# Where in a step the maxima are transposed: one reordering in a fused attention and gated-MLP kernel

## The chip, the cores and the metric

The kernel runs on one core of one Trainium2 chip. The metric is the time of one execution on the device, in microseconds (us), as the median of several runs. A profile is one further execution, recorded instruction by instruction. The engines of the core are named as the profile names them: PE is TensorE (matmuls; PEld is its loading of weights), DVE is VectorE, ACT is ScalarE, POOL is GpSimd, and SP is SyncE, which here only issues DMAs.

## What is computed

Two layers run one after the other, for 8 batches of 576 tokens. The first is a linear attention with 8 heads of 64 channels and 128 learned features, whose features are exponentials made stable by the largest absolute projection of each token. The second is a gated MLP, whose gate mixes the tokens of a batch with a 576 x 576 matrix. This is the reference, cut to its core:

```python
def phi(x):
    proj = np.einsum('bhsd,df->bhsf', x, w_phi)
    proj = proj - np.max(np.abs(proj), axis=-1, keepdims=True)
    return np.concatenate([np.exp(proj), np.exp(-proj)], axis=-1)
q_p, k_p = (phi(q), phi(k))
kv = np.einsum('bhsf,bhsd->bhfd', k_p, v)
z = np.sum(k_p, axis=2)
num = np.einsum('bhsf,bhfd->bhsd', q_p, kv)
den = np.einsum('bhsf,bhf->bhs', q_p, z)[..., None] + 1e-06
attn = num / den            # then heads are joined: x is (8, 576, 512)
...
h = np.maximum(x @ w_in, 0.0)
u, v = (h[..., :d_ff // 2].copy(), h[..., d_ff // 2:].copy())
v_n = (v - mu) / np.sqrt(var + 1e-06)          # mean and variance over channels
v_s = np.einsum('ts,bsd->btd', w_spatial, v_n) + b_spatial[None, :, None]
out = (u * v_s) @ w_out
```

## The kernel before

**Units and steps.** The work of the attention is cut into 36 units. 32 of them are pairs of heads of one batch (4 pairs for each of 8 batches), over the first 512 tokens. The last 64 tokens of a batch, its tail, are handled for two batches at once; such a tail unit holds all eight heads of both batches, and there are four. The program is software-pipelined: `step(i)` runs one stage each of several units. `LAGS` says how many steps after its own number a unit reaches a stage: keys and queries in its own step, the maxima's transpose one step later, features and sums two steps later, attention three, output four. `at_work(what)` finds the units that are due, and `run` calls the stage's functions for them.

**The stages that matter here.**

- `p_queries` projects the queries token by token into two PSUM tiles `pq`, and `r_queries` (line 299) reduces them to the maxima `mq`. GpSimd splits each maximum into a high and a low bf16 part in `mhl` (lines 304 and 305; in the first five units VectorE does it).
- `a_max_t` (line 334) transposes `mhl` on TensorE into a PSUM tile `pt`, and VectorE copies that to `mT` (line 337), so that the maxima lie along the free dimension.
- `p_features` (line 257) starts the feature tiles `pf`: eight small matmuls spread the negative maxima from `mT` with the selection matrix `sel`, and two larger ones add the projected queries. `e_features` (line 277) turns `pf` into `qf` with four exponentials on ACT.
- `p_keys`, `r_keys` and `e_keys` do the like for the keys: `pk`, the maxima `mk` (line 286) and the exponentials `kf` (line 291). `a_scale` makes `em` and, on GpSimd, the scaled values `vs`.
- `a_kv` sums keys times values (`pv<-vs,kf`, 20 matmuls), `a_num` multiplies features with these sums (`pn`) and normalizes them to `x` (lines 359 and 360), and `a_x_t` transposes `x` to `xT`, by TensorE for the first and last units and by DMA for the others.

**The second layer** comes in tasks, which `b_tasks` lists for a finished batch: `b_v` and `b_v_tail` (value half of the MLP, with its statistics), `b_ln`, `b_u` and `b_u_tail` (gate half), `b_s` and `b_s_tail` (mixing of tokens; the eviction multiplies into `uT` or, for the tail, `uTt`, lines 495 and 510), and `b_o` and `b_o_tail` (output projection `po`, evicted to `ob` at line 517 and stored). The tasks wait in a queue, and `fill(0.25)` takes some of them at four places of each step. What is left when the steps are over is run as a drain.

**What sets the order.** From step 8 on (`STRICT`), TensorE's instructions keep the order of the program; before that, and on the other engines throughout, the framework's scheduler orders them. All PSUM tiles come from one pool of eight, and each needs the eviction of an earlier tile of its bank. In a step of the kernel before, the features' matmuls come first, and the maxima's transpose for the next step's features is the last thing; the two stand next to each other in TensorE's queue.

All PE instructions carry the line of one helper, line 62, in the profile, so they are told apart by the names of their tiles.

Of the kernel before, what the change touches and what calls it, by code (L numbers as in the profile page):

```python
# [16 lines left out]
def kernel(  # L17
# [41 lines left out]
    strict = [False]  # L59
# [139 lines left out]
    def transpose_spatial(i):  # L199

        pt = psum.tile([P, S], BF16, tag="bank", name="pt")
        if i < NB:
            sc = POS[i]
            for tp, c in enumerate(POS):
                transpose(out=pt[:, tp * P:(tp + 1) * P], in_=wsp[:, c, bass.ds(sc, P, step=NB)],
                                    identity=ident)
            transpose(out=pt[:, T0:S], in_=wspt[:, bass.ds(sc, P, step=NB)],
                                identity=ident[:TL, :TL])
            nc.vector.tensor_copy(out=w_spT[:, i, :], in_=pt)
            return  # L210
        for bl in range(2):
            lo = bl * TL
            for tp, c in enumerate(POS):
                transpose(out=pt[lo:lo + TL, tp * P:(tp + 1) * P], in_=wspr[:, c, :], identity=ident)
            transpose(out=pt[lo:lo + TL, T0:S], in_=wspt[:, T0:S], identity=ident[:TL, :TL])
            nc.vector.tensor_copy(out=w_spT[lo:lo + TL, NB + bl, :], in_=pt[lo:lo + TL, :])
        for bl, row in ((0, TL), (1, 0)):
            r = slice(row, row + 1)
            pin(nc.scalar.copy)(
                out=w_spT[r, NB + bl, 0:T0].rearrange("o (a b p) -> o a b p", a=2, b=2),  # L220
                in_=bsp_row[r, 0:T0].rearrange("o (p b a) -> o a b p", a=2, b=2))
            pin(nc.scalar.copy)(out=w_spT[r, NB + bl, T0:S], in_=bsp_row[r, T0:S])
# [215 lines left out]
    def b_v(b, j):  # L438
        d = st[b]
        if j == 0:  # L440
            d["vn"] = s2.tile([P, NB, HALF], BF16, tag="vn", name="vn", bufs=2)
            d["uT"] = s2.tile([P, KC, T0], BF16, tag="uT", name="uT", bufs=2)
            d["mv"] = small.tile([P, NB, 2], FP32, tag="mv", name="mv")
            d["vr"] = {}
        d["vr"][j] = s2.tile([P, HALF], BF16, tag="vr", name="vr", bufs=5)
        stats = small.tile([P, 6], FP32, tag="stats", name="stats")
        v_mm(lambda kc: d["xT"][:, kc, j * P:(j + 1) * P], d["vr"][j], slice(0, P), stats, d["mv"][:, j, :])

    def b_ln(b):
        d = st[b]  # L450
        rstd = root(d["mv"], slice(0, P), NB)
        for j in range(NB):
            normalize(d["vn"][:, j, :], d["vr"][j], rstd[:, j, :])

    def b_v_tail(g, bls):
        d = gs[g]
        r = slice(bls[0] * TL, (bls[-1] + 1) * TL)
        vr = s2.tile([P, HALF], BF16, tag="vr", name="vr", bufs=5)
        stats = small.tile([P, 6], FP32, tag="stats", name="stats")
        mv = small.tile([P, 1, 2], FP32, tag="mv_t", name="mv_t")  # L460
        v_mm(lambda kc: d["xTt"][:, kc, r], vr, r, stats, mv[:, 0, :])
        rstd = root(mv, r, 1)
        for bl in bls:
            r = slice(bl * TL, (bl + 1) * TL)
            normalize(vnt[g % 2][r, bl, :], vr[r], rstd[r, 0, :])

    def b_u(b, dc):
        d = st[b]
        pu = psum.tile([P, T0], FP32, tag="bank", name="pu")
        for kc in range(KC):  # L470
            matmul(out=pu, lhsT=w_in_bf[:, kc, dc * P:(dc + 1) * P], rhs=d["xT"][:, kc, :],
                             start=(kc == 0), stop=(kc == KC - 1))
        nc.scalar.activation(out=d["uT"][:, dc, :], in_=pu, func=AF.Relu, bias=0.0, scale=1.0)

    def b_u_tail(g, bls):
        d = gs[g]
        if "uTt" not in d:
            d["uTt"] = s2.tile([P, KC, P], BF16, tag="uTt", name="uTt")
        r = slice(bls[0] * TL, (bls[-1] + 1) * TL)
        pu = psum.tile([P, KC, P], FP32, tag="bank", name="pu")  # L480
        for dc in range(KC):
            for kc in range(KC):
                matmul(out=pu[:, dc, r], lhsT=w_in_bf[:, kc, dc * P:(dc + 1) * P],
                                 rhs=d["xTt"][:, kc, r], start=(kc == 0), stop=(kc == KC - 1))
        nc.scalar.activation(out=d["uTt"][:, :, r], in_=pu[:, :, r], func=AF.Relu, bias=0.0, scale=1.0)
# [26 lines left out]
    def o_mm(lhs, r):  # L512
        po = psum.tile([P, DM], FP32, tag="bank", name="po")
        for dc in range(KC):
            matmul(out=po[r], lhsT=lhs(dc), rhs=w_out_bf[:, dc, :], start=(dc == 0), stop=(dc == KC - 1))
        ob = s2.tile([P, DM], FP32, tag="ob", name="ob", bufs=4)
        (nc.scalar.copy if drain[0] else nc.vector.tensor_copy)(out=ob[r], in_=po[r])  # L517
        return ob

    def b_o(b, j):  # L520
        ob = o_mm(lambda dc: st[b]["uT"][:, dc, j * P:(j + 1) * P], slice(0, P))
        dst = bass.AP(tensor=out.tensor, offset=out.offset + b * S * DM + POS[j] * DM, ap=[[NB * DM, P], [1, DM]])
        nc.sync.dma_start(out=dst, in_=ob)

    def b_o_tail(g, bls):
        r = slice(bls[0] * TL, (bls[-1] + 1) * TL)
        ob = o_mm(lambda dc: gs[g]["uTt"][:, dc, r], r)
        for bl in bls:
            nc.sync.dma_start(out=out[2 * g + bl, T0:S, :], in_=ob[bl * TL:(bl + 1) * TL, :])
# [20 lines left out]
    def b_tasks(b):  # L550

        g, bl = b // 2, b % 2
        alone = g in SPLIT
        bls = [bl] if alone else [0, 1]
        tail = alone or bl == 1
        mm = KC * T0 / 2400.0
        ms = (KC + 1) * T0 / 2400.0
        ts = []
        if tail:
            ts.append((mm, lambda: b_v_tail(g, bls)))  # L560
        ts += [(mm, lambda j=j: b_v(b, j)) for j in range(NB)]
        ts.append((0.0, lambda: b_ln(b)))
        if b == 0:
            ts += [(0.3, lambda i=i: transpose_spatial(i)) for i in range(NB + 1)]
        ts += [(mm, lambda dc=dc: b_u(b, dc)) for dc in range(KC)]
        if tail:
            ts.append((mm * len(bls) / 2, lambda: b_u_tail(g, bls)))
            for x in bls:
                ts += [(ms, lambda dc=dc, x=x: b_s(2 * g + x, dc)) for dc in range(KC)]
            ts.append((ms * len(bls) / 2, lambda: b_s_tail(g, bls)))  # L570
            ts.append((mm, lambda: b_o_tail(g, bls)))
            for x in bls:
                ts += [(mm, lambda j=j, x=x: b_o(2 * g + x, j)) for j in range(NB)]
        return ts

    RATE = 3.35
# [5 lines left out]
    def fill(share):  # L582
        credit[0] = min(credit[0] + RATE * share, CAP)
        while queue and credit[0] >= queue[0][0] / 2:
            cost, task = queue.pop(0)
            task()
            credit[0] -= cost
# [3 lines left out]
    def lag(u, what):  # L591
        return (FT if u["i"] == 1 else FIRST if u["pair"] and u["b"] == 0 else LAGS).get(what, 0)

    def step(i):

        if i == 0:
            a_transpose(units[0])

        def at_work(what):
            return [u for u in units[max(0, i - 5):i + 2] if u["i"] + lag(u, what) == i  # L600
                    and (u["pair"] or what not in ("sums", "attention", "out"))]

        def run(what, *fs):
            for u in at_work(what):
                for f in fs:
                    f(u)

        strict[0] = i >= STRICT
        run("features", p_features)
        run("keys", p_keys)  # L610
        run("queries", p_queries)
        run("features", e_features)
        run("keys", r_keys, lambda u: e_keys(u, 0))
        fill(0.25)
        run("queries", r_queries)
        run("keys", lambda u: e_keys(u, 1), a_scale)
        fill(0.25)
        for u in at_work("attention"):
            a_num(u)
            if u["pj"] == NP - 1:  # L620
                finish_batch(u, tail_num)
        fill(0.25)
        run("sums", a_kv)
        run("next", a_transpose)
        fill(0.25)
        for u in at_work("out"):
            a_x_t(u)
            if u["pj"] == NP - 1:
                finish_batch(u, tail_x_t)
                queue.extend(b_tasks(u["b"]))  # L630
        run("maxima", a_max_t)

    def finish_batch(u, f):
        g, bl = u["g"], u["b"] % 2
# [70 lines left out]
```

## Time and profile before

| what | value |
| --- | --- |
| time, median of 3 runs | 322.27 us (321.13 to 323.19) |
| span of the profiled execution | 320.2 us |
| granted TensorE clock, mean | 0.952 |
| PE, DVE, ACT, POOL busy | 79%, 68%, 67%, 56% |
| transposes of the maxima, mean | 36 of 225 ns |
| copies to `mT`, median | 36 of 211 ns |
| exponentials `qf<-pf` | 144 of 618 ns |

Busy shares are means over a program with several stages: loads and the first steps up to about 55 us, the main loop to about 276 us, and a drain after it. For a change in the order of instructions, the waits tell more than the shares: which engine stood idle, ahead of which instruction, and whose result ended that. The start of `pf` marks the start of a step in the timeline, so that the trace can be cut there and each step be read by itself.

The profile shows the exponentials of the features like this (busy us, mean ns of one, then the idle time of ACT just before them and what ended it):

```profile
L277 ACT ACTIVATE qf<-pf 128x512 bf16<-128x512 f32 x144 | 74.8, 618 | 61.3 <-PE pf L62 61.3
```

### The profile page before, as it was taken

To read this page: it belongs to the slowest core of one execution; us is meant where nothing else is said; L and a number is where in the kernel's file an instruction comes from. 1 tells how busy PE (TensorE), PEld (TensorE's weight loads), DVE (VectorE), ACT (ScalarE), POOL (GpSimd) and SP (SyncE) were. 2 spreads that over 40 slices of the span, in tenths; PEclk is the share of its full clock that TensorE was granted. 3 is DMA by queue.
4 is the path that set the end of the run, shared out by engine and by line. 5 is a ranking of instruction groups with operands and counts; after the bars stand their busy time and mean duration, and the time that the engine had idled before them with its cause. 6 is when DMAs were issued, how large, how long until landed. Compare 5 with 4: busy or idle time off the path is not lost.

```text
span 320.2 us, 8370 instructions
## 1 busy us (share of the span) xinstructions
PE 253.0 (79%) x3270; PEld 158.3 (49%) x3270; DVE 217.3 (68%) x538; ACT 215.3 (67%) x488; POOL 180.6 (56%) x320
## 2 busy tenths in 40 slices
PE   2174768989788697987787888858988878999984
PEld 1063656556445354654654556534455545644541
DVE  4377786876757765878777778857777674875420
ACT  5667876879535786878898867745989853256123
POOL 8259578487513569437968983643598640018400
PEclk9999797979959899999899999998999999999999
DMA  7959999941907729997990899599700000520017
GB/s 194 212 100 185 205 211 128 145 133 14 121 17 194 87 51 218 137 264 179 112 165 18 188 151 191 147 266 230 101 19 18 16 18 23 203 74 2 0 42 253
DMA packets 81707, 40.32 MB, mean 126 GB/s; under 512 B 50243, under 2 KB 77059, under 8 KB 81669
## 3 DMA queue, kind: packets, MB, share of 16 engines
q1 hardware_dynamic: 54180, 28.32, 40.1%
q0 software_dynamic: 27328, 11.41, 31.6%
q8 instruction: 25, 0.41, 0.6%
q14 instruction: 14, 0.11, 0.1%
q10 hardware_dynamic: 160, 0.07, 0.1%
HBM read 32.85 MB, written 9.44 MB: 132 GB/s over the span
## 4 chain that ended last, share of the span: by engine, by line
PE 42%; DVE 23%; ACT 20%; DMA 7%; issue 4%; POOL 3%; SPq 0%; DVEq 0%; ACTq 0%; POOLq 0%
PE ps L62 11%; ACT qf L277 10%; PE pf L62 7%; PE pv L62 7%; PE po L62 6%; ACT kf L291 6%; PE pu L62 5%; DVE stats L421 4%; DMA q_tl<-in_q_dram 4%; DMA out_dram<-ob 3%; DVE mk L286 3%; DVE x L360 3%; PE pn L62 2%; DVE ob L517 2%; DVE uT L495 2%
## 5 line engine op out<-in xcount | busy, mean ns | idle before, releaser
L277 ACT ACTIVATE qf<-pf 128x512 bf16<-128x512 f32 x144 | 74.8, 618 | 61.3 <-PE pf L62 61.3
L315 POOL TENSOR_TENSOR vs<-v_f,em 128x512 bf16<-128x512 f32 x64 | 65.9, 1042 | 50.3 <-ACT em L310 48.7
L291 ACT ACTIVATE kf<-pk 128x512 bf16<-128x512 f32 x144 | 79.3, 663 | 4.3 <-DVE mk L286 4.2
L286 DVE TENSOR_REDUCE mk<-pk 128x4 f32<-128x512 f32 x72 | 46.4, 686 | 36.5 <-PE pk L62 34.3
L62 PE MATMUL pf<-mT,sel 64*128 64x128 bf16 x288 | 15.6, 232 | 39.7 <-DVE mT L337 38.4
L299 DVE TENSOR_REDUCE mq<-pq 128x4 f32<-128x512 f32 x62 | 40.5, 680 | 0.1
L62 PE MATMUL ps<-w_spT,vn 128*128 128x512 bf16 (+1 forms) x256 | 38.8, 286 | 1.4 <-POOL vn L435 1.0
L62 PEld LDWEIGHTS <-sel 64*128 64x128 bf16 x288 | 10.2, 99 | 47.6 <-DVE mT L337 28.3
L421 DVE BATCH_NORM_STATS2 stats<-vr 128x6 f32<-128x512 bf16 (+1 forms) x37 | 25.0, 684 | 11.9 <-ACT vr L420 11.7
L62 PE MATMUL pv<-w_in_bf,xT 128*128 128x512 bf16 x128 | 32.7, 395 | 0.0
L495 DVE TENSOR_TENSOR uT<-ps,uT 128x512 bf16<-128x512 f32 x32 | 21.9, 686 | 15.6 <-PE ps L62 13.9
L62 PE MATMUL po<-w_out_bf,uT 128*128 128x512 bf16 x128 | 32.2, 392 | 0.0
L62 PE MATMUL pu<-xT,w_in_bf 128*128 128x512 bf16 x128 | 31.7, 382 | 0.0
L420 ACT ACTIVATE vr<-pv 128x512 bf16<-128x512 f32 (+1 forms) x37 | 23.0, 665 | 10.4 <-PE pv L62 10.1
L62 PEld LDWEIGHTS <-kf 128*128 128x128 bf16 x640 | 25.5, 102 | 6.1 <-issue 0.6
L62 PEld LDWEIGHTS <-qf 128*128 128x128 bf16 (+1 forms) x640 | 24.1, 102 | 8.2 <-issue 1.7
L62 PE MATMUL pn<-kv,qf 128*128 128x66 bf16 (+1 forms) x640 | 26.0, 197 | 0.6 <-ACT qf L277 0.5
L62 PE MATMUL pv<-vs,kf 128*128 128x66 bf16 x512 | 26.3, 200 | 0.1
L517 DVE COPY ob<-po 128x512 f32<-128x512 f32 (+1 forms) x28 | 18.9, 685 | 9.4 <-PE po L62 7.0
L360 DVE TENSOR_TENSOR x<-pn,rc 128x256 bf16<-128x256 f32 x64 | 25.0, 417 | 0.4
L330 POOL TENSOR_TENSOR vst<-v_tl,em 64x512 bf16<-64x512 f32 x16 | 16.4, 1038 | 15.1 <-ACT em L310 14.8
L435 POOL TENSOR_SCALAR vn<-vr,rs 128x512 bf16<-128x512 bf16 x32 | 24.2, 769 | 0.7
(106 smaller groups left out, 456.6 us busy)
## 6 DMA issues: line engine op xcount, KB each, us to landing
v_f<-in_v_dram SPq DMA_DIRECT2D x8, 1024.0 KB, 8.3
out_dram<-ob SPq DMA_DIRECT2D x32, 256.0 KB, 2.5
k_bf<-in_k_dram POOLq DMA_DIRECT2D x7, 512.0 KB, 7.7
q_bf<-in_q_dram POOLq DMA_DIRECT2D x7, 512.0 KB, 7.3
v_tl<-in_v_dram SPq DMA_DIRECT2D x8, 128.0 KB, 6.5
w_in_bf<-in_moe_w_in_dram POOLq DMA_DIRECT2D x2, 512.0 KB, 8.2
out_dram<-ob SPq DMA_DIRECT2D x8, 128.0 KB, 2.3
k_tl<-in_k_dram POOLq DMA_DIRECT2D x8, 64.0 KB, 5.1
```

The lines of the kernel that those rows point to most:

```text
L62: r = f(*a, **kw)
L277: nc.scalar.activation(out=qf[:, s, 4 * par:4 * par + 4, :], in_=u["pf"][par], func=AF.Exp, bias=0.0, scale=sc)
L286: nc.vector.tensor_reduce(out=mk[:, par, :], in_=u["pk"][par], axis=AX.X, op=ALU.max, apply_absolute_value=True)
L291: nc.scalar.activation(out=u["kf"][:, s, 4 * par:4 * par + 4, :], in_=u["pk"][par], func=AF.Exp, bias=0.0, scale=sc)
L299: nc.vector.tensor_reduce(out=mq[:, 4 * par:4 * par + 4], in_=pq[par], axis=AX.X, op=ALU.max, apply_absolute_value=True)
L315: nc.gpsimd.tensor_tensor(out=vs[:, s, :, 0:D], in0=st[u["b"]]["v"][:, pj * H:(pj + 1) * H, :], in1=em[:, s, :].unsqueeze(2).to_broadcast( ...
L360: nc.vector.tensor_tensor(out=x, in0=pn[r, :, 0:D], in1=rc[r].to_broadcast([n, 4, D]), op=ALU.mult)
L420: nc.scalar.activation(out=dst[r], in_=pv[r], func=AF.Relu, bias=0.0, scale=1.0)
L421: nc.vector.bn_stats(out=stats[r], in_=dst[r])
L435: nc.gpsimd.tensor_scalar(out=dst, in0=src, scalar1=rs[:, 0:1], scalar2=rs[:, 1:2], op0=ALU.mult, op1=ALU.add)
L495: nc.vector.tensor_tensor(out=d["uT"][:, dc, :], in0=ps, in1=d["uT"][:, dc, :], op=ALU.mult)
L517: (nc.scalar.copy if drain[0] else nc.vector.tensor_copy)(out=ob[r], in_=po[r])
```

## The change

There are three edits, all of them in the order in which work is issued; no arithmetic changes.

1. From step 8 on, `a_max_t` is issued ahead of `a_kv`, after the third `fill`, and no longer at the end of the step. In the first eight steps it stays at the end. This puts other work between the transpose and the features that need it.
2. In the first eight steps `p_features` and `e_features` run late in the step, after `a_kv` and `a_transpose`, and not at its beginning. From step 8 on they stay where they were.
3. In `b_tasks` the tail's output projection moves from ahead of all the output projections to just before the last two of them, so that it does not directly follow the eviction it reads.

```diff
             ts.append((ms * len(bls) / 2, lambda: b_s_tail(g, bls)))
-            ts.append((mm, lambda: b_o_tail(g, bls)))
             for x in bls:
                 ts += [(mm, lambda j=j, x=x: b_o(2 * g + x, j)) for j in range(NB)]
+            ts.insert(len(ts) - 2, (mm, lambda: b_o_tail(g, bls)))
         return ts
...
         strict[0] = i >= STRICT
-        run("features", p_features)
+        if strict[0]:
+            run("features", p_features)
         run("keys", p_keys)
         run("queries", p_queries)
-        run("features", e_features)
+        if strict[0]:
+            run("features", e_features)
         run("keys", r_keys, lambda u: e_keys(u, 0))
...
         fill(0.25)
+        if strict[0]:
+            run("maxima", a_max_t)
         run("sums", a_kv)
         run("next", a_transpose)
+        if not strict[0]:
+            run("features", p_features, e_features)
         fill(0.25)
         for u in at_work("out"):
             a_x_t(u)
             if u["pj"] == NP - 1:
                 finish_batch(u, tail_x_t)
                 queue.extend(b_tasks(u["b"]))
-        run("maxima", a_max_t)
+        if not strict[0]:
+            run("maxima", a_max_t)
```

## The prediction

> **What bounds the kernel now.** I read the page's busy shares first, then the sums of waits, then one step boundary in the timeline, then a table of the main loop cut at its step boundaries.
>
> ```profile
> span 320.2 us, 8370 instructions
> ...
> PE 253.0 (79%) x3270; PEld 158.3 (49%) x3270; DVE 217.3 (68%) x538; ACT 215.3 (67%) x488; POOL 180.6 (56%) x320
> ```
>
> No engine is full over the span. TensorE (PE) is the busiest, so the question is what its idle fifth, 67 us, waits for. The sums of waits say (engine, what waited, who ended it: us in total, times, longest):
>
> ```profile
> ACT qf L277 <- PE pf L62: 61.3, 32, 6.4
> ...
> PE pf L62 <- DVE mT L337: 38.4, 35, 3.5
> ...
> DVE mk L286 <- PE pk L62: 34.3, 32, 1.9
> ...
> PE po L62 <- DVE uTt L510: 3.0, 3, 1.9
> ...
> PE pt L62 <- ACT qf L277: 0.8, 2, 0.6
> ```
>
> One row holds more than half of TensorE's idle time: `pf`, the first matmuls of a step, waits for `mT`, 35 times out of 36. ACT and VectorE (DVE) then wait in their turn for what TensorE starts at that point (61.3 and 34.3 us). So once a step all three large engines stand still together. Waits for a PSUM bank are small, as the last row shows. The timeline at one boundary (start us, duration, engine, line, what):
>
> ```profile
> 169.10 0.22 PE L62 MATMUL pt<-ident,mhl 128*128 128x128 bf16 x1
> ...
> 170.03 0.66 DVE L421 BATCH_NORM_STATS2 stats<-vr 128x6 f32<-128x512 bf16 x1
> ...
> 170.83 0.19 DVE L337 COPY mT<-pt 128x128 bf16<-128x128 bf16 x1
> 171.08 0.40 PE L62 MATMUL pf<-mT,sel 64*128 64x128 bf16 x8 [1.75 <-DVE mT L337]
> ```
>
> The transpose of the maxima is TensorE's last instruction of the step; its result goes through VectorE's queue behind other work, and TensorE's next instruction needs it. Where VectorE was free the round trip still cost 0.32 us (at 152.00 and 177.23). Some rows of the table cut at the starts of `pf` (stretch, length, then busy us of each engine):
>
> ```profile
> core 0: us, PE busy (x) PEld busy (x) DVE busy (x) ACT busy (x) POOL busy (x), PEclk, DMA share, GB/s
> 81.94:92.12 10.18, 7.70 (x97) 4.61 (x98) 7.16 (x18) 4.20 (x10) 3.58 (x8) 0.84 0.47 62
> 161.77:171.08 9.31, 7.56 (x88) 4.28 (x89) 7.12 (x19) 8.43 (x22) 6.09 (x15) 1.00 0.70 115
> 184.04:190.56 6.52, 5.59 (x78) 3.39 (x79) 5.38 (x12) 4.47 (x11) 5.78 (x11) 1.00 1.70 140
> 204.51:213.82 9.31, 5.80 (x79) 3.58 (x79) 6.05 (x13) 4.58 (x11) 6.97 (x13) 1.00 0.94 252
> ```
>
> Length minus TensorE's busy time is close to the wait that ends each row (6.52 - 5.59 = 0.93, wait 0.93). The second row warns: ACT has 8.43 of 9.31 us to do there, so the 1.75 us cannot all come back.
>
> [...]nothing but the release of `mT` holds `pf` at 171.08. [...]the copy of `mT` waits behind a statistic 0.66 us long, and no later matmul passes the waiting `pf`. [...]
>
> **The change, part by part.**
>
> *Maxima in the middle of the step (from step 8 on).* It adds nothing: the same 0.22 us transpose and the same 0.21 us copy. In the built program the transpose stands just ahead of the kv sums, with 20 matmuls, about one queue task and, on some steps, the transposes of `x` or of a tail still to come before the next `pf`. From the timeline the stretch from the sums to the step's end is 1.6 us or more (201.75 to 203.24), against a round trip of 0.3 to 1.0 us. On VectorE the copy now mostly stands ahead of the last PSUM eviction of the step. The input `mhl` is ready: it is written by GpSimd in the step before (149.35 to 149.82 for a transpose that would run past 155). The moved transpose waits for a PSUM bank that an eviction of `pk` or `pq` frees; that is the same wait that the kv sums met at this place before, and it was nearly empty, so I cost it at nothing. What is queued behind it on TensorE is the sums, and behind them the step's end.
>
> From 55.15 to 270.72 the table has 29 steps, 215.57 us, and their closing waits add up to 31.9 us. For each step I took the larger of (length - wait) and (VectorE's or ACT's busy time, whichever is larger, + 0.5 us). The 0.5 us is my choice[...]. It gives back 20.1 us. With 0 us it is 26.9, so the sum does not hang on the choice. Examples: 184.04 returns 0.64 of 0.93; 161.77 returns 0.38 of 1.75; 204.51 returns 2.76 of 3.50, if the output stores that held VectorE there move along; 152.00 returns nothing.
>
> *Features late in steps 2 to 7.* The six waits there (20.25 to 48.32) add to 7.1 us (1.21+1.31+0.67+2.17+1.01+0.68). `pf` no longer heads the step, so `pk` follows the transposes at once and VectorE, which paces these steps, goes on. VectorE's work is 4.5 to 4.8 us in the steps at 37.02 and 42.83 that last 5.81 and 5.49. Half the 7.1 us, 3.5, seems safe: VectorE's copies of `kT`, `qT` and `xT`, and TensorE's wait for `x` (1.42 and 0.99 us at 30.11 and 47.19), stay. At the switch to step 8 ACT has eight exponentials of `qf` in a row instead of four, 2.06 us more ahead of `kf`, in a step where ACT (7.31) and VectorE (8.06 of 9.85) are nearly full: -1.5 us.
>
> *Tail output projection between the others.* `po` of the tail followed the eviction that makes `uTt` directly: 3.0 us in three waits (1.89 at 88.97, 0.85 at 307.83, the rest short). Other projections, 1.03 us each when warm, now fill them. +2.7 us; the number of stores is the same.
>
> Sum: 20.1 + 3.5 - 1.5 + 2.7 = 24.8 us; 322.3 - 24.8 = 297.5, called 297. A warmer clock is left out of it. The drain from 276 on, 44 us, is otherwise untouched.
>
> **The rivals.**
>
> *All of it returns.* 31.9 + 7.1 + 3.0 = 42.0 us would give 280; less the 1.5 us of the switch and the 5.0 us that the fullest steps keep even with 0 us added (31.9 - 26.9), 35.5 us and about 286. [...] Against: ACT has 5.30 of 5.30 us in the step at 152.00.
>
> *VectorE and ACT become the bound.* VectorE's busy time is 6.05 against TensorE's 5.80 in the step at 204.51, and 5.38 against 5.59 at 184.04. If each step keeps about half of its wait under another name (a bank not yet evicted, `vn` from GpSimd, which has 8.03 us of rough busy time in the step at 116.74), the loop gives 10 us and the rest 2: 310.
>
> *No gain, or slower.* The transposing DMAs set the pace instead: `kT_b` and `qT_b` of one batch are issued at 100.30 and 102.21, `qT_b` takes a median of 5.8 us to land and is needed at about 109.4, a little over 1 us later. If every batch were like that, the waits would only move to `pk` and the time stay at 320 to 322; with a bad order in the first eight steps and the eight exponentials it would be 326. Against it: the same sum leaves some 2 us for the batch issued at 157 and over 3 us for those at 131, 190 and 221, and TensorE waits for no transposed tile in the loop now.
>
> **How the numbers follow.** Forecast near 297 (292 to 303): 0.58. All returns, near 286: 0.17. Half is taken by others, near 310: 0.16. No change 0.04, slower 0.05. So faster by over 1% has 0.91. The range runs from 285, which takes in most of the second case, to 311, which takes in most of the third.
>
> **What would show it.** Right: the row of `pf` waiting for `mT` falls from 38.4 us to under 6, ACT's wait for `pf` from 61.3 to about 35, TensorE's share rises to 85% or so, steps such as the one at 184.04 last near 5.9 us, and `po` no longer waits for `uTt`. Wrong: new rows of some 10 us or more at `pt`, `pv` or `pf` released by ACT or VectorE, or at `pk` released by a DMA, or first steps as long as before (5.3 to 6.8 us).

## The result, and the profile after

The changed kernel takes 296.43 us (median of 4; 294.33 to 301.70) against 322.73 for the kernel before on the same chip: a ratio of 0.9158, with a 95% interval of 0.9073 to 0.9244. The forecast was 297.0. The first recorded execution of the changed kernel was a slow one, at 301.7 us, so the profile read below is that of a second execution, at 296.37 us.

The busy shares and the span of the page, changed kernel:

```profile
span 294.5 us, 8327 instructions
...
PE 247.6 (84%) x3229; PEld 154.5 (52%) x3270; DVE 216.6 (74%) x538; ACT 215.7 (73%) x488; POOL 180.8 (61%) x320
```

VectorE, ACT and GpSimd do what they did (217.3, 215.3 and 180.6 us before), in a span that is 25.7 us shorter. TensorE's 253.0 have become 247.6 us; its weight loads number 3270 in both, and 41 of the new trace's matmul records are missing, so this drop is not exact. The sums of waits, changed kernel (engine, what waited, who ended it: us in total, times, longest):

```profile
ACT qf L277 <- PE pf L62: 30.1, 22, 5.1
...
DVE mk L286 <- PE pk L62: 13.2, 17, 2.1
...
PE pf L62 <- DVE mT L337: 9.6, 9, 3.6
DVE ob L517 <- DMA out_dram<-ob: 6.7, 2, 3.6
...
PE pt L62 <- POOL mhl L305: 2.0, 1, 2.0
...
PE pq L62 <- DMA qT_b<-q_bf: 1.2, 1, 1.2
...
PE pt L62 <- ACT kf L291: 0.3, 1, 0.3
```

The row that held more than half of TensorE's idle time went from 38.4 us in 35 waits to 9.6 in 9, and with it fell the rows of ACT (61.3 to 30.1) and VectorE (34.3 to 13.2), which in the main passed the same stall on. The row of `po` waiting for `uTt` is gone. Two rows matter that were small or absent: VectorE waits 6.7 us, in two pieces, for an output buffer `ob` whose store has not landed (2.3 us before), and TensorE waits for a transposed tile from DMA.

The boundary that the prediction showed at 169.10, in the changed kernel's timeline:

```profile
154.27 0.22 PE L62 MATMUL pt<-ident,mhl 128*128 128x128 bf16 x1
...
154.33 0.29 PE L62 MATMUL pv<-vs,kf 128*128 128x66 bf16 x4
...
154.96 1.02 PE L62 MATMUL pu<-xT,w_in_bf 128*128 128x512 bf16 x3
...
155.87 0.21 DVE L337 COPY mT<-pt 128x128 bf16<-128x128 bf16 x1
...
156.13 0.40 PE L62 MATMUL pf<-mT,sel 64*128 64x128 bf16 x8
```

The trip through VectorE is as slow as it was: the transpose starts at 154.27 and the copy at 155.87, 1.60 us later, against 1.73 before (169.10 to 170.83). Over the 29 steps of the loop this distance even grew, from 1.06 us in the mean to 1.46. The change did not make the trip shorter; it put the sums and other queue tasks over it, and `pf` starts with no wait in brackets.

The table cut at the starts of `pf`, changed kernel (stretch, length, then busy us of each engine). The first, fourth, fifth and sixth rows are the four steps that the prediction showed; the second and third are two that went wrong:

```profile
core 0: us, PE busy (x) PEld busy (x) DVE busy (x) ACT busy (x) POOL busy (x), PEclk, DMA share, GB/s
73.55:80.72 7.17, 6.23 (x99) 4.22 (x98) 7.08 (x19) 4.20 (x10) 4.50 (x9) 1.00 1.09 141
92.56:102.20 9.64, 7.53 (x77) 4.01 (x80) 6.75 (x18) 7.48 (x18) 6.45 (x13) 0.82 0.28 60
121.65:131.62 9.97, 5.91 (x79) 3.56 (x80) 6.36 (x17) 6.16 (x14) 4.08 (x9) 1.00 1.02 226
146.83:156.13 9.30, 8.88 (x87) 4.78 (x88) 7.57 (x20) 8.26 (x22) 6.67 (x15) 0.82 0.78 119
168.17:173.78 5.61, 5.56 (x77) 3.37 (x79) 5.38 (x12) 4.47 (x11) 5.61 (x10) 1.00 2.38 169
186.32:195.76 9.44, 5.75 (x78) 3.54 (x79) 5.92 (x13) 4.58 (x11) 7.58 (x13) 0.97 0.92 272
```

The step of 6.52 us now lasts 5.61, of which TensorE works 5.56: it became the bound of this step. The step of 10.18 lasts 7.17, at full clock instead of 0.84. The step of 9.31 at 161.77 stayed at 9.30: its wait of 1.75 us is gone, but TensorE's own work took 8.88 us at a clock of 0.82, against 7.56 at 1.00. The one at 204.51 stayed too (9.44). The two others grew, from 7.74 and 7.29 us.

The timeline of the last row shows what still stops all engines (SPq is SyncE's queue of DMA issues):

```profile
188.25 3.03 SPq L523 DMA_DIRECT2D out_dram<-ob  x4
...
190.41 0.22 PE L62 MATMUL pt<-ident,mhl 128*128 128x128 bf16 x1
...
194.89 0.69 DVE L517 COPY ob<-po 128x512 f32<-128x512 f32 x1 [3.08 <-DMA out_dram<-ob]
195.50 0.21 DVE L337 COPY mT<-pt 128x128 bf16<-128x128 bf16 x1
195.76 0.61 PE L62 MATMUL pf<-mT,sel 64*128 64x128 bf16 x8 [3.64 <-DVE mT L337]
```

The maxima were transposed at 190.41, five us ahead of their use, and still `pf` waited 3.64 us: VectorE stood idle for 3.08 us ahead of an eviction into an `ob` buffer that a store still held (194.89), and copied `mT` only after it, at 195.50. A wait that names `mT` is here a wait for a DMA, two steps back in the chain. The stores of 256 KB in this stretch (180 to 200 us) took a median of 6.5 us to land, against 2.5 over the whole program; a load of 1 MB was issued on the same queue just ahead, at 187.63, and loads of `k_bf` and `q_bf` and DMA transposes fall into the stretch too. Whether any of them slowed the stores, and which, is not shown.

Summed by stretch, on the profiles (us):

| stretch | before | after | saved | forecast |
| --- | --- | --- | --- | --- |
| up to step 8 | 55.15 | 50.27 | 4.9 | 3.5 |
| the 29 steps of the loop | 215.57 | 195.55 | 20.0 | 20.5 (20.1 - 1.5 + the 1.89 stall of `po`) |
| the rest | 49.5 | 48.7 | 0.8 | 0.85 (the stall of `po` at 307.83) |

### The profile page after: what moved, and what is told of

It is laid out like the page before. It is cut to its first block, busy times and chain, and to the rows that moved or that the text cites. A ratio compares the mean times of both kernels' runs of the same rounds, so it can differ in the third digit from the quotient of the medians.

```text
span 299.8 us, 8368 instructions
## 1 busy us (share of the span) xinstructions
PE 253.3 (84%) x3270; PEld 155.7 (52%) x3270; DVE 216.9 (72%) x538; ACT 215.3 (72%) x488; POOL 180.4 (60%) x320
## 3 DMA queue, kind: packets, MB, share of 16 engines
HBM read 32.85 MB, written 9.44 MB: 141 GB/s over the span
## 4 chain that ended last, share of the span: by engine, by line
PE 50%; ACT 19%; DMA 10%; DVE 9%; POOL 7%; issue 3%; SPq 0%; DVEq 0%; POOLq 0%; ACTq 0%
PE ps L62 11%; PE pv L62 10%; ACT qf L277 10%; PE po L62 9%; PE pf L62 5%; ACT kf L291 5%; PE pu L62 5%; DMA out_dram<-ob 4%; DMA q_tl<-in_q_dram 4%; PE pn L62 3%; PE pt L62 3%; DVE stats L421 2%; POOL vn L435 2%; DMA qT_b<-q_bf 2%; PE pk L62 2%
## 5 line engine op out<-in xcount | busy, mean ns | idle before, releaser
L286 DVE TENSOR_REDUCE mk<-pk 128x4 f32<-128x512 f32 x72 | 46.4, 684 | 13.0 <-PE pk L62 12.4
L62 PEld LDWEIGHTS <-kf 128*128 128x128 bf16 x640 | 24.7, 101 | 7.7 <-issue 4.9
L62 PE MATMUL pf<-mT,sel 64*128 64x128 bf16 x288 | 16.9, 232 | 11.5 <-DVE mT L337 10.6
L62 PEld LDWEIGHTS <-vn 128*128 128x128 bf16 x256 | 16.2, 98 | 13.9 <-POOL vn L435 1.8
```

Of the source, the lines that this page charges most:

```text
L62: r = f(*a, **kw)
L286: nc.vector.tensor_reduce(out=mk[:, par, :], in_=u["pk"][par], axis=AX.X, op=ALU.max, apply_absolute_value=True)
```

## The experiments

"Saved" below is one minus the ratio, times the time of the kernel before in the same comparison (321.9 to 322.8 us).

### Each edit alone

The first: the maxima's transpose moved as in the change, nothing else.

```diff
         fill(0.25)
+        if strict[0]:
+            run("maxima", a_max_t)
         run("sums", a_kv)
...
-        run("maxima", a_max_t)
+        if not strict[0]:
+            run("maxima", a_max_t)
```

> Only the first edit: the maxima transposed ahead of the kv sums from step 8 on. Theory A (the round trip from TensorE over VectorE and back was the cost): the row of pf waiting for mT falls from 38.4 us to about 7 us, which is what the first steps keep, and the time falls by 20 us to about 302 (the share that the prediction gave this edit). Theory B (the first steps bring as much as the main loop): at most 10 us from this edit, 312 or more. Theory C (a warmer TensorE clock brings much of it): the time falls below 299 and the granted clock rises above 0.97.

Measured: 305.0 us, ratio 0.9419 (0.9360 to 0.9477): 18.7 us saved. Its sums of waits:

```profile
PE pf L62 <- DVE mT L337: 15.2, 13, 5.8
...
DVE ob L517 <- DMA out_dram<-ob: 8.1, 2, 5.3
```

This edit alone takes 23.2 of the 38.4 us out of the row, and alone it brings up the wait for `ob` (2.3 to 8.1 us). The mean granted clock of this profile, 0.954, is that of before (0.952), and TensorE's busy time fell by 3.9 us (253.0 to 249.1), so in this profile, as an estimate, a warmer clock is no more than about a fifth of the saving (3.9 of 18.7 us).

The second: features late in steps 2 to 7, with the switch at step 8.

```diff
-        run("features", p_features)
+        if strict[0]:
+            run("features", p_features)
...
-        run("features", e_features)
+        if strict[0]:
+            run("features", e_features)
...
+        if not strict[0]:
+            run("features", p_features, e_features)
         fill(0.25)
```

> Only the second edit: features late in the first eight steps. Theory A: 2 us (3.5 saved in steps 2 to 7, 1.5 lost at the switch to step 8), about 320. Theory B: 8 us or more, below 315, since pf starts step 8 about 4.7 us earlier in the changed kernel than in the one before (50.50 against 55.15) and step 9 about 5.8 us earlier (59.22 against 65.00).

Measured: 317.89 us, 0.9852 (0.9809 to 0.9894): 4.8 us saved. The step of the switch:

```profile
49.71:59.56 9.85, 8.21 (x102) 5.10 (x102) 8.06 (x22) 8.01 (x19) 4.49 (x11) 1.00 1.00 150
```

Before, step 8 lasted 9.85 us as well (55.15 to 65.00). So the eight exponentials in a row, costed at 1.5 us, cost nothing there. They start at 48.39, 1.3 us ahead of the step. And the first steps gave more: from the first transposes of `q_bf`, which a load releases (17.36 here, 18.32 before), to step 8 it is 32.35 us against 36.83, 4.5 us less where 3.5 was forecast. Why they gave more is not shown.

The third: the tail's projection between the others.

```diff
-            ts.append((mm, lambda: b_o_tail(g, bls)))
             for x in bls:
                 ts += [(mm, lambda j=j, x=x: b_o(2 * g + x, j)) for j in range(NB)]
+            ts.insert(len(ts) - 2, (mm, lambda: b_o_tail(g, bls)))
```

> Only the third edit: the tail's output projection just before the last two of the others. Theory A: the 3.0 us that po waits for uTt go, and the time falls by 2.7 us, to about 320. Rival: these waits only move to the mT wait that follows them at the step's end, since VectorE has the same evictions to do, and the time stays within 1 us of before.

Measured: 318.3 us, 0.9864 (0.9817 to 0.9912): 4.4 us saved, 2.8 to 5.9. The two steps around the old stall of 1.89 us, in this kernel:

```profile
81.55:89.64 8.09, 6.28 (x98) 4.23 (x99) 7.08 (x18) 4.20 (x10) 3.59 (x8) 1.00 0.52 68
89.64:96.55 6.91, 6.08 (x72) 3.44 (x71) 5.62 (x11) 4.47 (x11) 2.03 (x3) 1.00 0.36 120
```

Before, they lasted 10.18 and 8.36 us, at clocks of 0.84 and 0.79. The prediction shows the first of them; this is the second, in the kernel before:

```profile
92.12:100.48 8.36, 7.52 (x71) 4.35 (x71) 5.72 (x11) 4.58 (x11) 2.49 (x5) 0.79 0.32 110
```

So the two are 3.5 us shorter. The stall of 1.89 us at `po` is gone, but `pf` at the end of the same step now waits 1.81 us for `mT`, where it waited 0.59:

```profile
89.64 0.40 PE L62 MATMUL pf<-mT,sel 64*128 64x128 bf16 x8 [1.81 <-DVE mT L337]
```

Of the 1.89 us, 1.22 came back there, as the rival has it, and the waits give only 0.7 us. The other 2.8 us are TensorE's own work: 7.70 + 7.52 = 15.2 us before and 6.28 + 6.08 = 12.4 here. Before, the clock fell from 1.00 to 0.50 as the stall ended and stayed there from 88.9 to 95.7 us; in this kernel a pause of nearly the same length, 1.81 us, came just ahead of 89.64, and the clock stayed at 1.00. These traces do not show what decides. Slow windows also move about: in this same profile another step ran at 0.69 and took 10.99 us, 9.61 before.

The smaller stall, 0.85 us in the drain, was saved in full: from the last `pf` to the end it is 48.6 us, 49.5 before. But another 1.8 us of the 4.8 by which this profile is shorter lie ahead of the first `pf` (18.45, 20.25 before), where this edit changes nothing. So the time refutes the rival's "within 1 us", while its mechanism held at the largest stall; how much of the 4.4 us is the edit and how much the clock stays open.

The three savings add up to 27.9 us; together they gave 27.2 (0.0842 x 322.73). Within their intervals no interaction shows.

### Another engine for the copy

In the kernel before, ACT instead of VectorE copies the maxima; the order stays.

```diff
-        nc.vector.tensor_copy(out=mT[u["i"] % NM], in_=pt)
+        nc.scalar.copy(out=mT[u["i"] % NM], in_=pt)
```

> The kernel before with one edit of another kind: ACT copies the transposed maxima to mT instead of VectorE, and the order of the steps stays. ACT stands idle ahead of pf for 61.3 us in 32 steps of before, so its queue is mostly empty when the transpose ends. If it is VectorE's queue that makes the round trip long, the wait of pf falls from 1.1 us a step to 0.4 or 0.5 us (the bare round trip was 0.32 us), 20 us in all, and the time to about 303 to 308. If the bare distance between the two matmuls is the cost, whatever copies, the wait stays near 1 us a step and the time within 3 us of before.

Measured: 316.14 us, 0.9767 (0.9714 to 0.9820): 7.5 us saved, well short of what I had expected. Its rows:

```profile
PE pf L62 <- ACT mT L337: 31.0, 36, 3.2
...
DVE ob L517 <- DMA out_dram<-ob: 7.3, 2, 4.0
```

All 36 steps still wait, with a new releaser. In 15 of them ACT stood idle ahead of the copy, and there the wait is 0.35 to 0.41 us: even with an empty queue the trip costs some 0.4 us a step. In the other 21 ACT had other work ahead, and the wait reaches 3.2. I had taken ACT's queue for mostly empty at that point, and it is not. The store stalls are here too: VectorE's waits for a store rose from 2.3 to 7.3 us, and TensorE stood 5.1 us for banks whose evictions they held, so the shortfall is not ACT's alone. With the copy on ACT 7.5 us come back, with distance in TensorE's queue 18.7.

### How far ahead

Two kernels vary the place of the transpose in the changed kernel: later (after the sums) and earlier (ahead of `r_queries`, at the first `fill`). The changed kernel was run again beside them.

```diff
# later
-        if strict[0]:
-            run("maxima", a_max_t)
         run("sums", a_kv)
+        if strict[0]:
+            run("maxima", a_max_t)
         run("next", a_transpose)
```

```diff
# earlier
+        if strict[0]:
+            run("maxima", a_max_t)
         fill(0.25)
         run("queries", r_queries)
...
-        if strict[0]:
-            run("maxima", a_max_t)
         run("sums", a_kv)
```

> The changed kernel with the transpose of the maxima just after the kv sums instead of just ahead of them; one queue task, at most about 1 us of matmuls, stands between it and the next pf. Theory A (what counts is the distance to pf against a round trip of 0.3 to 1.0 us, more where VectorE is behind): waits of pf on mT come back in part, 3 to 8 us in sum over the loop, and the time is 2 to 6 us longer, 298 to 302. Rival: any distance will do, and the time stays within 1 us of the changed kernel.

> The changed kernel with the transpose of the maxima moved further forward, ahead of the first queue task of the step. Theory A (once the round trip is covered, nothing is left to gain): no faster, and slower where mhl is not ready yet, since GpSimd writes it 3.9 us and later into the step before and TensorE would wait in order; 296 to 303. Rival: still earlier helps, by the remaining waits of pf on mT outside the first steps, to 292.

> The changed kernel once more, for a second profile: 294 to 298 us. The first profile has one stall of 6.2 us at pf near 201 us, ahead of which VectorE waits for an output store to free its buffer (5.8 us at the longest). If that stall is part of the kernel's order of stores, it is there again with some length; if it is a chance of that execution, it is absent.

Measured: later 300.22 us, 0.9294 (0.9229 to 0.9360); as in the change 296.25, 0.9198 (0.9136 to 0.9259); earlier 296.95, 0.9164 (0.9089 to 0.9240). The later place saves 3 us less by the point values; the intervals overlap a little, so this is likely and not certain. In its profile (an execution of 302.24 us) the waits have come back in part:

```profile
PE pf L62 <- DVE mT L337: 17.8, 12, 6.4
```

Without the longest wait of each, a store stall, it is 11.4 us against 6.0 in the change. The earlier place can't be told from the change. In its profile (298.71 us) no `pf` inside the loop waits for `mT`; another row has come up:

```profile
PE pt L62 <- POOL mhl L305: 6.9, 7, 1.9
```

Too early, the transpose meets its own input, which GpSimd has not finished. Once the trip was covered, more distance only moved the wait to the other end of it.

The second profile of the changed kernel answers its question: the stall of 6.2 us near 201 us is there again, with 3.64 us at 195.76, and the profile of the first edit alone has it with 5.8. So it is no chance of one execution: with this order it recurs, and its length varies.

### The new wait for output buffers

Six `ob` buffers instead of four, in the changed kernel and, as a control, in the kernel before:

```diff
-        ob = s2.tile([P, DM], FP32, tag="ob", name="ob", bufs=4)
+        ob = s2.tile([P, DM], FP32, tag="ob", name="ob", bufs=6)
```

The tile `first`, which shares the tag, has its count changed alike.

> The changed kernel with six output buffers ob instead of four. Theory A (the stores, queued behind the transposing DMAs in SyncE's queue, became the next wait once the steps are shorter): VectorE's wait for out_dram, 10.4 us in the first profile, falls below 2 us, the longest waits of pf and pv on VectorE go, and the time falls by 5 to 8 us, to 288 to 291. Theory B (these waits are covered, since the engines are full elsewhere): within 2 us of the changed kernel.

> The kernel before with six output buffers instead of four, as a control. Theory A (the stores became a wait because the steps got shorter): VectorE waits for a store 2.3 us in before and is released early in the rest, so this kernel gains 1 to 2 us at most, under half of what the buffers give the changed kernel. Rival (the buffers are worth the same with either order): 4 us faster than before, near 318.

Measured: 292.33 us, 0.9067 (0.9004 to 0.9130), with six buffers on the change, some 4.2 us better than the change in the same comparison (0.0131 x 322.42). The control: 318.32, 0.9886 (0.9842 to 0.9930), 3.7 us. In the changed kernel with six buffers the wait of VectorE for `out_dram` has left the list, and the longest wait of `pf` fell from 3.6 to 2.0 us:

```profile
PE pf L62 <- DVE mT L337: 7.4, 9, 2.0
```

So a part of the lost gain was held by these buffers. But my theory that this wait is a product of the shorter steps falls: the kernel before gains nearly as much from the same two buffers. Its step at 204.51, whose wait of 3.50 us was such a stall, went from 9.31 to 6.87 us in the control's profile, 2.4 of the 3.7; where the rest comes from is open.

Next, the stores on ACT's DMA queue, with four buffers, and then both together:

```diff
-        nc.sync.dma_start(out=dst, in_=ob)
+        nc.scalar.dma_start(out=dst, in_=ob)
```

The two stores of the tail (line 529) are changed alike.

> The changed kernel, four buffers, with the output stores issued from ACT's queue instead of SyncE's. Theory A (a store is late because it is queued behind DMA transposes in one queue): VectorE's wait for out_dram falls below 2 us, as with six buffers. What the time does depends on ACT[...]: 292 if ACT has room there, 300 or more if its exponentials are held back. Rival (the stores are late because the DMA engines themselves are full): the wait for out_dram stays near 7 us.

> The changed kernel with both: the stores issued from ACT's queue and six output buffers. Theory A (both edits remove the same wait, VectorE's for a buffer): not additive, a ratio to before between 0.900 and 0.908, like each alone (0.904 and 0.907). Rival (the queue also delays the DMA transposes behind the stores, and the buffers remove something else): additive, a ratio near 0.892 and a time near 287 us.

Measured: 291.98 us, 0.9043 (0.8988 to 0.9098), for the queue alone; 291.93, 0.9006 (0.8955 to 0.9057), with six buffers too. The changed kernel shows at its stall of 121.65 to 131.62 why the queue matters:

```profile
115.76 6.22 SPq L74 DMA_TRANSPOSE kT_b<-k_bf  x1
...
122.42 2.98 SPq L74 DMA_TRANSPOSE qT_b<-q_bf  x1
125.49 1.01 SPq L523 DMA_DIRECT2D out_dram<-ob  x2
...
128.02 0.69 DVE L517 COPY ob<-po 128x512 f32<-128x512 f32 x1 [3.61 <-DMA out_dram<-ob]
128.77 0.29 PE L62 MATMUL pv<-vs,kf 128*128 128x66 bf16 x4 [2.80 <-DVE ob L517]
```

Four evictions into `ob` were made at 117.86 to 121.84, but SyncE was busy issuing two transposing DMAs, and the first of their stores left at 125.49. With the stores on ACT's queue they leave at 118.31 to 122.30, each right after its eviction, and this step, 121.39 to 127.13 there, lasts 5.74 us instead of 9.97. The row for `out_dram` is down to 1.4 us. But the next step of that profile lasts 10.34 us instead of 5.75, at a clock of 0.83, with a new wait in it:

```profile
PE pq L62 <- DMA qT_b<-q_bf: 2.8, 1, 2.8
```

So at this place the gain went straight to the next wait, that for a transposed tile, and to the clock: the two steps together last 16.08 us, 15.72 in the changed kernel. What this profile gains lies elsewhere: 3.2 us at the second stall, and 2.8 in the step at 92.56, which ran at 0.82 in the changed kernel and at 1.00 here, with 1.5 of it lost again in the step behind. At the first stall, in the changed kernel, the issue of the two transposes took 9.2 us of SyncE's time (6.22 and 2.98), and the stores stood behind it. The second stall (186.32 to 195.76) is of another kind: there the stores left some 2 us after their evictions (185.46 and 188.25 for the first), and then took long to land (a median of 6.5 us, as above).

The two remedies overlap: together they are not told apart from either alone. By ratio all three versions beat the changed kernel, by 4 to 6 us against its 0.9198 and by 3 to 5 against its first comparison (0.9158); only the six buffers were run beside it.

### The transposing DMAs a step earlier

With six buffers, the DMA transposes of `k` and `q` are issued three steps ahead of their use instead of two:

```diff
-    AT, AB, XP = 4, 5, 2
+    AT, AB, XP = 4, 5, 3
```

> The changed kernel with six output buffers and with the DMA transposes of the keys and queries of a batch (kT_b and qT_b) issued a step earlier, three steps ahead of their first use instead of two. Theory A (in the step at about 93 us TensorE waits for these two, 0.8 to 1.0 and 1.2 us, since shorter steps ate their lead): both waits go, and the time falls by 2 us against six buffers alone, to about 290. Rival: the earlier transposes push output stores and transposes of x back in the same queue, new waits on DMAs take the place, and the time stays or grows by up to 3 us.

Measured: 298.74 us, 0.9241 (0.9182 to 0.9299): worse than with six buffers alone (0.9067), by 5.6 us in ratio, more than the rival's 3. The waits for `kT_b` and `qT_b` are gone, 1.9 us in sum in the changed kernel and 2.2 with six buffers, but in their stead stands:

```profile
PE pv L62 <- DMA xT<-x: 8.5, 3, 3.8
```

The transposes of `x` share SyncE's queue, and now TensorE waits for them, 8.5 us in sum: here the longer lead for the one came with a loss for the other. TensorE's own work in the loop is longer too, 177.2 us against 171.4, at a granted clock of 0.962 in the mean of the profile against 0.974; how much of the loss is that stays open.

## Why the prediction was right, point by point

**The bound, and edit 1 (20.1 us forecast).** Right: 18.7 measured alone. The reading was that one round trip through VectorE, at a place where TensorE has nothing else, stops three engines. The trace after shows the same trip, as long as ever, with work over it. What was sized too small is the trip: 0.3 to 1.0 us was set against a stretch of 1.6 or more (1.49 by the two times given, 201.75 and 203.24). From the transpose to the copy it was already 1.06 us in the mean before, with 3.45 at the longest, and 1.46 after. So nine waits are left.

**The rule for the steps.** Right in the mean and wrong in places; its 0.5 us was my estimate. The step at 184.04 was to last 5.88 us and lasts 5.61; the one at 161.77 was to give back 0.38 us and gave 0.01, for TensorE ran at 0.82 in it; the one at 152.00 (5.30) was to give nothing and lasts 5.29. The 2.76 us of the step at 204.51 did not come: "if the output stores move along" was the step of the working that failed. They did not, and the stores cost a further 2.7 us at the step that began at 138.59. The row "`ob` waits for `out_dram`" was small in the page of before, but its one wait (2.28 us, ahead of the eviction at 212.27) held up the copy of `mT` behind it, at 213.55. The rule gives 195.5 us for the 29 steps and the trace 195.55, but that is cancellation, and so luck: the steps at 109.00, 138.59 and 204.51 lasted 8.6 us longer than the rule says, and the three from 81.94 to 109.00 5.3 shorter.

**What made up for it.** The three steps from 81.94 to 109.00 lasted 27.06 us before and last 19.01. TensorE's waits for `mT` and `uTt` explain 5.0 us of these 8.05 (0.59 + 0.83 + 2.60 + 1.89, less the 0.89 that `pf` still waits at 80.72). Its busy time there fell from 21.14 to 17.90 us, with the clock at 1.00 in all three, after 0.84 and 0.79 in two of them: the warmer clock, which the sum had left out. Six steps of the loop ran below 0.9 before, three after. That fewer stalls brought this is not shown.

**`mhl` is ready.** Mostly: one wait of 2.0 us remains, in the shortest step (4.17 us).

**The moved transpose's bank wait, costed at nothing.** Right for the transpose itself: 0.3 us in one wait. The sums just behind it waited 2.8 us once, at 128.77, for a bank whose eviction a store held up.

**Edit 2 (3.5 - 1.5 = 2.0 us forecast).** Measured 4.8, with an interval of 3.4 to 6.2. Both terms were off the same way: the first steps gave about 4.5, not half the waits' 7.1 us but nearly two thirds, and the switch cost 0.

**Edit 3 (2.7 us forecast).** Measured 4.4 (2.8 to 5.9). The waits of `po` went, but not all of their time: of the 1.89 us at 88.97, 1.22 came back at `mT`, as the rival said. That the total is no less than the forecast came in part from the clock in the two steps shown, and the prediction had no term for it.

**The sum.** 24.8 forecast and 27.2 measured by the ratio. That they lie so close is partly luck: stores and DMA leads took back what the clock and the first steps added. In the loop the waits for `mT` fell by 22.8 us (31.9 to 9.1) and TensorE's own work by 7.3 (178.6 to 171.3), 30.1 in all; only 20.0 came out, so about 10 us are idle time under other names. It is a rough sum, since missing matmul records count as idle in it.

**The rivals.** "All of it returns" (286; its sum gives 286.8): not reached; even with stores out of the way the best stands near 292. "VectorE and ACT become the bound" (310): no; but the step at 152.00 shows ACT full, as it said. "No gain", by the lead of the transposing DMAs: its mechanism did happen, in the one batch that it named. The step from 109.00 grew from 7.74 to 9.64 us, with 0.8 us at `kT_b` and 1.2 at `qT_b`; the other batches had lead enough in this profile.

**What would show it.** The row of `pf` fell to 9.6, not under 6; ACT's row to 30.1, lower than the 35 forecast; TensorE's share to 84%. In the first row 3.64 us are the store stall at 195.76, about the whole miss; but with six buffers, where VectorE waits for no store in the loop, the row is still 7.4, so the trip itself left more than forecast.

## What to carry to other kernels

When one engine's last instruction of a step feeds its own first instruction of the next through another engine, move the pair apart in the queue until other work covers the trip (18.7 us here); look for the wait that stops all engines at once, and price each step by what its next-fullest engine leaves. Stop when the trip is covered: placed earlier than that here, the moved instruction waited for its own input (6.9 us in seven waits). And before trusting a step to return its wait, read who stands ahead of the copy in its queue: here an eviction held up by a store (3.08 us at 194.89) kept the stall under the copy's name, and one held up by stores behind a slow issue (3.61 us at 128.02, after 2.98 of issuing from 122.42) cost 2.80 us at `pv` and 1.21 more under that name.

## What the hardware showed that was not expected

- SyncE was occupied for 6.22 and 2.98 us by the issue of two transposing DMAs (5.03 and 4.56 for the same two with the stores on ACT's queue), and the first store behind them left at 125.49, its eviction having begun at 117.86; on ACT's queue, each issue of a 256 KB store there took 0.34 us.
- With nothing ahead of the copy, TensorE still waited 0.35 to 0.41 us for a trip through ACT, and, in the kernel before, 0.32 through VectorE (at 152.00 and 177.23).
- Stores of 256 KB landed in a median of 2.5 us over the program and of 6.5 us in the stretch from 180 to 200 us, beside a load of 1 MB and other transfers.
- As a stall of 1.89 us ended, in the kernel before, the granted clock fell from 1.00 to 0.50 and stayed there for 6.8 us (88.9 to 95.7). After a pause of 1.81 us at the same place, with the third edit alone, it did not, nor in the step after the stall at 121.65 to 131.62 (waits of 2.80 and 1.21 us, clock 1.00).
